# Products of ones beside the small products, another order in the first layer, and a longer ring

## The chip, the core and the metric

The kernel runs on one core of one Trainium2 chip. The core has TensorE (PE in the profile; its weight loads are PEld), VectorE (DVE), ScalarE (ACT), GpSimd (POOL) and SyncE (SP), which issues most transfers. Results of TensorE land in eight banks of PSUM. The metric is the device time of an execution in microseconds, from the first to the last instruction and a little around it; lower is better.

## The reference

Agent attention over B = 4 batches of N = 11,456 tokens with C = 128 channels and 49 agents, followed by a mixture of E = 8 experts with F = 1,024 hidden units, of which each token uses the one with the largest gate.

```python
s = scale * (agents @ k.T);  a2k = softmax(s over tokens);  agent_v = a2k @ v      # 49 x 128 per batch
x = softmax(scale * (q @ agents.T) over agents) @ agent_v                          # N x 128 per batch
logits = x @ w_gate;  e = argmax(logits)
out = softmax(logits)[e] * sigmoid(x @ w_output_gate)[e] * (relu(x @ w1[e]) @ w2[e])
```

All of it is fp32.

## The kernel before, in words

Tokens are worked on in units of 1,024 (11 per batch and a last one of 192); a unit is up to eight blocks of 128 tokens. Three kinds of **small products** in fp32 stand for the attention, eight to a unit: `ks` (key scores, block by agents, 50 columns), `av` (the weighted sum of v, accumulated over a unit) and `qs` (query scores). After the last `ks` of a batch the maximum over tokens is found (`km_t`, `km_r`), the weights `ev` of a unit are made by a subtraction on DVE or POOL and an exponential on ACT, and `av` follows. After the last `av`, `fold` finds the expert that most tokens of the batch will take (product `ga`, index `ei`), fetches its w1 and w2 (`w1t`, `w2t`), multiplies the agents' values by w1 (`aw`) and splits the result into fp16 parts `w`; `gates` makes the gate's weights (`bn`, `g`, then `lg` per unit).

The **main stream** goes over 92 tiles of up to 512 tokens. The first layer, `mm1(i, hf)`, makes four of a tile's eight chunks of 128 hidden units, one in each of PSUM banks 0 to 3 (G4 = 4), as fp16: a full product of 128 rows (`own_`, against the turned query weights x1) and a product of the 19 rows that are left (`rest`, against x2). The four small ones sit at partitions 0, 32, 64 and 96 and so run side by side in TensorE's row groups. `relu` brings a chunk out of its bank: ACT writes hh (fp16 of the ReLU), DVE writes hl (the rest of it), and the bank is released. hh and hl are rings of `RING` buffers each. The second layer, `mm2(i, k, f)`, multiplies hh and hl of chunk f by w2 into a bank y; `finish` and `store` sum and store it.

The order is made when the program is built. A model clock (`Clock`) holds a time for each engine; streams (generators) wait until their next instruction fits, and `tick(heavy, light)` lets at most `heavy` fp32 and `light` other TensorE instructions of the streams in. `main_stream` chooses between `mm1` and `mm2`: `mm2` when the first layer is more than `OFF` chunks ahead, `mm1` when banks 0 to 3 are free and the ring has room. Before the first `mm1` (`clk.started` false) and in gaps `idle` runs: it ticks, and it issues a filler, a product of fp16 ones into a free bank (`warm`), while the columns that the model has streamed in the last 3,413 ns are under a limit. The model counts an fp32 column four times:

```python
            n = _free(outs[0]) * (4 if ins[0].dtype == F32 and ins[0].shape[0] else 1)
            self.recent.append((t + cost, n * ins[0].shape[0] / 128.0))
```

At the start 36 fillers are issued outright. Loads of k, q and v go to `LARGE` places of 4 KB per partition; the turned weights x1 and x2 go to `SMALL` places of their own, or to large ones while more than `KEEP` of those are free. All instructions are recorded by one helper, so the profile gives them line 193.

Of the kernel before, what the change touches and what calls it, by code (L numbers as in the profile page):

```python
# [16 lines left out]
P = 128  # L17
# [3 lines left out]
UNITS = [(u * 1024, 128, 8) for u in range(11)] + [(11264, 96, 2)]  # L21
# [3 lines left out]

YS = 2

LARGE, SMALL, KEEP = 10, 8, 5
PHASES = [(0, 3, 13, 384), (3, 1, 1, 128)]
NG = B * E  # L30
BIG = 1048576.0
# [3 lines left out]
G4 = 4  # L35
# [207 lines left out]
def agent_attention_top1_moe(ctx, tc, qT, kT, v, aT, wg, wo, w1, w2, cst, out):  # L243
    nc = tc.nc
    clk = Clock()
    ACT, DVE, POOL = Engine(clk, "ACT", nc.scalar), Engine(clk, "DVE", nc.vector), Engine(clk, "POOL", nc.gpsimd)
    PE, SY = Engine(clk, "PE", nc.tensor), Engine(clk, "SP", nc.sync)
# [17 lines left out]
    def n_free():  # L265
        return sum(banks[k][0] for k in others)
# [4 lines left out]
    def first_free():  # L271
        return min((when_free(banks[k]), k) for k in others if banks[k][0])

    def bank(name, dt=F32, w=512, k=None):

        k = last[0] = first_free()[1] if k is None else k
        t = ps.tile([P, w], dt, tag=f"b{k}", bufs=1, name=name)
        banks[k][1] = t.name
        return t

    def hold(long=False):

        k = last[0]
        banks[k][0] = False
        if long:
            long_held.append((k, banks[k][1]))
        return k
# [4 lines left out]
    def idle_bank():  # L292
        free = [(when_free(x), k) for k, x in enumerate(banks) if x[0]]
        return min(free)[1] if len(free) > 1 and min(free)[0] <= clk.now() else None

    def group_free():

        if not all(banks[k][0] for k in range(G4)):
            return None
        return max(when_free(banks[k]) for k in range(G4))  # L300

    def wait_free(long=False):
        while True:
            long_held[:] = [x for x in long_held if not banks[x[0]][0] and banks[x[0]][1] == x[1]]
            if n_free() > (1 if clk.started else 0) and not (long and len(long_held) > 1) and first_free()[0] <= clk.now() + 50.0:
                return
            yield None
# [8 lines left out]
    def load_constants():  # L316
        SY.dma_start(kc, cst)
        SY.dma_start(wgo[:, 0:E], wg)
        SY.dma_start(wgo[:, E:2 * E], wo)
        for t in gss:  # L320
            POOL.tensor_copy(t[:, 0, 16:17], own)
# [8 lines left out]
    own = kc[:, K_OWN:K_OWN + 1]  # L330
    dup = kc[:, K_DUP:K_DUP + 1]
    idle_x = cp.tile([P, 256], F16, name="idle_x")
    idle_w = idle_x[:, 0:P]
# [9 lines left out]
    for i in range(4):  # L343
        t = cp.tile([P, 8, P], F16, name=f"e16_{i}")
        e16s.append(t)
    avd = []
    for i in range(2):
        t = cp.tile([P, 2, P], F32, name=f"avd_{i}")
# [3 lines left out]
    for i in range(2):  # L352
        t = cp.tile([P, 2, 18], F16, name=f"gs_{i}")
# [3 lines left out]
    for i in range(2):  # L357
        t = cp.tile([P, E, NCOL], F32, name=f"oht_{i}")
# [63 lines left out]
    mains = [0]  # L422
# [4 lines left out]
    def spawn(g, prio=2):  # L427
        streams.append([prio, len(streams), g, None])
        streams.sort(key=lambda x: x[0])

    def tick(heavy=1, light=2):

        clk.slots = [heavy, 0]
        for x in list(streams):
            if x[3] is not None and x[3][0] == "PE" and clk.can(x[3], x[0]):
                step(x)
        clk.slots = [0, light]
        for x in list(streams):
            while x[2] is not None and (x[3] is None or clk.can(x[3], x[0])):
                step(x)  # L440
                if x[3] is None:
                    break
        streams[:] = [x for x in streams if x[2] is not None]

    def step(x):
        try:
            x[3] = next(x[2])
        except StopIteration:
            x[2] = x[3] = None

    def idle():
        t = clk.vt["PE"]
        tick(*((1, 2) if clk.started else (1, 4)))
        k = idle_bank()
        if mains[0] == 0 and clk.columns(t) < (WARM if clk.vt["PE"] == t else 3600) and k is not None:

            PE.matmul(bank("warm", k=k)[:, 0:P], idle_w, idle_w, start=True, stop=True)
        elif clk.vt["PE"] == t:
            clk.vt["PE"] += 40.0

# [28 lines left out]
    def scored(item):  # L489
        places[held.pop(item)][0] = True  # L490
# [16 lines left out]
    def loads():  # L507
        for n, item in enumerate(ITEMS):
# [5 lines left out]
            if n == 1:  # L514
                load_constants()

    def scores(item, name):
        kind, b, u = item
        base, pp, nt = UNITS[u]
        while item not in parts:  # L520
            yield None
        yield from wait_free(True)
        x = parts.pop(item)
        s = bank(name)
        mark = hold(True)
        for t in range(nt):
            yield from PE.q.matmul(s[0:pp, t * A2:(t + 1) * A2], x[:, t * pp:(t + 1) * pp], at[:, b, :], start=True,
                                   stop=True)
        scored(item)
        return s, mark  # L530

# [77 lines left out]
    def v_unit(b, u):  # L609
        base, pp, nt = UNITS[u]  # L610
        item = ("v", b, u)
        while b not in K or u not in K[b] or item not in parts:
            yield None
        if u == 0:
            K[b]["av"] = wk.tile([P, A2], F32, name=f"avs{b}", tag="avs")
        yield from wait_free()
        avp = bank(f"av{b}_{u}")
        mark = hold()
        avo = avp[:, 0:A2]
        x = parts.pop(item)  # L620
        e = K[b].pop(u)
        for t in range(nt):
            sl = slice(t * C, (t + 1) * C)
            last_ = t == nt - 1
            yield from PE.q.matmul(avo, x[0:pp, sl], e[:, t, :], start=(t == 0), stop=last_)
        scored(item)
        K[b]["v"] += 1
        if b == 0 and u == NU - 4:
            others[:] = range(G4, 8)
        spawn(v_rest(b, u, avo, mark))  # L630

    def v_rest(b, u, avo, mark):
        av = K[b]["av"]
        while K[b]["av_n"] < u:
            yield None
        if u == 0:
            yield from DVE.q.tensor_copy(av, avo)
        else:
            yield from DVE.q.tensor_tensor(av, av, avo, op=ALU.add)
        release(mark)  # L640
        K[b]["av_n"] += 1
        if u == NU - 1:
            spawn(fold(b), -1)
# [179 lines left out]
    def q_unit(b, u):  # L823
        s, mark = yield from scores(("q", b, u), f"qs{b}_{u}")
        spawn(q_rest(b, u, s, mark))
# [3 lines left out]
    def roomy(me, n):  # L829

        if me < n:
            return True
        b, u = tiles[max(mains[0] - 1, 0)][0:2]
        return NU * b + u > me - n and rests[me - n] > 1
# [146 lines left out]
    def small_products():  # L981
        for kind, b, u in ITEMS:
            while kind == "q" and not roomy(NU * b + u, AHEAD):
                yield None
# [6 lines left out]
            for h in range((nt + 3) // 4):  # L991
                tiles.append((b, u, h, pp, min(4, nt - 4 * h)))
    NT = len(tiles)
    OFF = 6
    RING = 12
    H = {}
    Y = {}
    done, summed = set(), set()

    def mm1(i, hf):  # L1000


        b, u, h, pp, n = tiles[i]
        w = pp * n
        own_, rest = state[b]["w"][hf]
        x1, x2 = (x[:, 512 * h:512 * h + w] for x in X1[b, u])
        p = []
        for g in range(G4):
            p.append((bank(f"h{i}_{hf}_{g}", k=g), hold()))
            rows = slice(32 * g, 32 * g + AR)  # L1010
            PE.matmul(p[g][0][:, 0:w], rest[rows, g * P:(g + 1) * P], x2[rows, :], start=True, stop=False)
        for g in range(G4):
            PE.matmul(p[g][0][:, 0:w], own_[:, g * P:(g + 1) * P], x1, start=False, stop=True)
            spawn(relu(i, G4 * hf + g, *p[g]), 0)
            if g == G4 - 1 and hf == 1 and 4 * h + n == UNITS[u][2]:
                for x in ("x1", "x2"):
                    scored((x, b, u))
            tick()

    def relu(i, f, p, mark):  # L1020
        b, u, h, pp, n = tiles[i]
        w = pp * n
        hh = wk.tile([P, 512], F16, name=f"hh{i}_{f}", tag="hh", bufs=RING)
        hl = wk.tile([P, 512], F16, name=f"hl{i}_{f}", tag="hl", bufs=RING)
        yield from ACT.q.activation(hh[:, 0:w], p[:, 0:w], AF.Relu)
        yield from DVE.q.scalar_tensor_tensor(hl[:, 0:w], p[:, 0:w], 0.0, hh[:, 0:w], op0=ALU.max, op1=ALU.subtract)
        release(mark)
        H[i, f] = hh, hl
# [52 lines left out]
    def main_stream():  # L1081
# [3 lines left out]
        while m2 < len(second_):  # L1085
            can1 = can2 = False
            now = clk.now()
            if m1 < len(first_) and G4 * (m1 + 1) - freed <= RING and group_free() is not None and group_free() <= now + 20.0:
                i, hf = first_[m1]
# [4 lines left out]
            if (i, f) in H:  # L1094
                vv = state[tiles[i][0]]["vv"]
                can2 = len(vv) > f // 4 and clk.at([H[i, f][1], vv[f // 4]]) <= now
                can2 = can2 and (f > 0 or n_free() > 1)
            if can2 and (G4 * m1 > NB * i + (NB * k + f) / (tiles[i][4] // 2) + OFF or not can1):
                mm2(i, k, f)
# [11 lines left out]
        while streams:  # L1111
            idle()
# [312 lines left out]
                return stop.value  # L1425

    AHEAD = 5
    WARM = 6000
    WARM0 = 36
    LOW = POOL  # L1430
# [79 lines left out]
```

## Time and profile before

| | |
|---|---|
| median of 3 runs | 1107.53 us (1099.12 to 1108.6) |
| the profiled execution | 1105.42 us |
| its span | 1103.7 us |
| busy: PE, PEld, DVE, ACT, POOL | 1062.5, 874.1, 869.6, 594.1, 273.6 us |
| mean granted TensorE clock | 0.954 |
| first main product (h) | 98.34 us from the start |

A row of a timeline gives start and length in us, the engine, the operation with output and inputs (buffer numbers left out), its shape and how many; in brackets the idle time ahead of it and who ended it. A row of a stretch gives its bounds and length, and for each engine the busy time and the instructions that touch it, then the granted clock as a share, the busy share of the DMA engines and GB/s. A row of waits names who waited for whom, the sum in us, how often, and the longest.

### The profile page before, as it was taken

How to read it: one execution, taken by the hardware profiler on the slowest of the kernel's cores; microseconds unless marked ns; L12 is line 12 of the kernel's file. 1: busy time of each engine (PE TensorE's matmuls, PEld its weight loads, DVE VectorE, ACT ScalarE, POOL GpSimd, SP SyncE). 2: the span in 40 equal slices, each digit the busy share in tenths (PEclk: the TensorE clock that was granted, in tenths of full speed). 3: DMA queues.
4: the chain of work that ended last, by engine and by line, in shares of the span. 5: the costliest groups of instructions: out<-in, count | busy, mean ns of one | idle time of the engine just before them, and what ended most of it. 6: DMA issues, size and time to landing. Idle time of an engine off the chain costs nothing. (4 is left out here: it accounts for less than half of the span.)

```text
span 1103.7 us, 27308 instructions
## 1 busy us (share of the span) xinstructions
PE 1062.5 (96%) x10516; PEld 874.1 (79%) x10516; DVE 869.6 (79%) x2344; ACT 594.1 (54%) x1396; POOL 273.6 (25%) x440
## 2 busy tenths in 40 slices
PE   9999979999999999999999999999899989999996
PEld 9997858787778878888688878877676767878885
DVE  2626869898988898988988899888987979857652
ACT  2205636556655565665655566566555545655552
POOL 0300213232112122322112222231122344621121
PEclk9557989999999999999999999999999989999998
DMA  9527683444536634445455544455212364545340
GB/s 345 180 31 285 167 145 121 112 136 133 158 88 158 183 105 118 147 127 150 119 145 166 161 113 121 112 166 149 60 45 74 52 168 69 144 137 167 124 123 29
DMA packets 108817, 147.11 MB, mean 133 GB/s; under 512 B 61128, under 2 KB 71548, under 8 KB 108682
## 3 DMA queue, kind: packets, MB, share of 16 engines
q1 hardware_dynamic: 107338, 143.83, 46.6%
q0 software_dynamic: 1344, 1.49, 0.8%
q8 instruction: 83, 1.36, 0.5%
q14 instruction: 52, 0.43, 0.1%
HBM read 91.86 MB, written 35.17 MB: 115 GB/s over the span
## 5 line engine op out<-in xcount | busy, mean ns | idle before, releaser
L193 PE MATMUL y<-vv,hh 128*128 128x256 f16 (+1 forms) x2880 | 585.3, 275 | 8.8 <-DVE os L193 3.7
L193 PE MATMUL y<-vv,hl 128*128 128x128 f16 (+1 forms) x2880 | 531.0, 220 | 0.1
L193 DVE SCALAR_TENSOR_TENSOR hl<-h,hh 128x512 f16<-128x512 f32 (+1 forms) x736 | 447.4, 666 | 91.9 <-ACT hh L193 91.2
L193 ACT ACTIVATE hh<-h 128x512 f16<-128x512 f32 (+1 forms) x736 | 373.2, 590 | 230.9 <-PE h L193 229.5
L193 PEld LDWEIGHTS <-hl 128*128 128x128 f16 (+1 forms) x2880 | 318.3, 111 | 16.8 <-issue 4.3
L193 PEld LDWEIGHTS <-hh 128*128 128x128 f16 (+1 forms) x2880 | 290.4, 101 | 48.6 <-issue 3.2
L193 PE MATMUL h<-x_ld,w 19*128 19x512 f16 (+1 forms) x1472 | 296.0, 382 | 7.6 <-DVE hl L193 7.3
L193 PEld LDWEIGHTS <-w 19*128 19x128 f16 x1472 | 91.0, 102 | 111.8 <-issue 86.4
L193 POOL TENSOR_TENSOR os<-os,smt 128x512 f32<-128x512 f32 (+1 forms) x92 | 94.3, 1025 | 270.4 <-issue 213.5
L193 PE MATMUL av<-ev,v_ld 128*128 128x50 f32 x720 | 124.6, 287 | 0.0
L193 PEld LDWEIGHTS av<-ev,v_ld 128*128 128x128 f32 x720 | 122.4, 227 | 2.3 <-issue 1.0
L193 PEld LDWEIGHTS qs<-at,q_ld 128*128 128x128 f32 x720 | 116.3, 200 | 8.1 <-issue 0.3
L193 PE MATMUL qs<-at,q_ld 128*128 128x50 f32 x720 | 116.1, 256 | 0.3 <-DVE s_s L193 0.2
L193 PE MATMUL ks<-at,k_ld 128*128 128x50 f32 x720 | 106.3, 259 | 0.0
L193 PEld LDWEIGHTS ks<-at,k_ld 128*128 128x128 f32 x720 | 104.6, 196 | 1.9 <-issue 0.3
L193 ACT COPY ys<-y 128x256 f32<-128x256 f32 x180 | 68.0, 378 | 50.9 <-PE y L193 50.0
L193 DVE TENSOR_TENSOR os<-y,ys 128x256 f32<-128x256 f32 x180 | 74.6, 414 | 22.3 <-ACT ys L193 13.3
L193 POOL TENSOR_TENSOR e<-ef,e 128x392 f16<-128x392 f32 (+1 forms) x48 | 41.6, 867 | 160.2 <-ACT e L193 150.8
L193 POOL TENSOR_TENSOR ev<-S,km_o 128x400 f32<-128x400 f32 (+1 forms) x44 | 40.4, 918 | 145.3 <-PE av L193 103.3
L193 POOL TENSOR_SCALAR smt<-lT,i 128x8 f32<-128x8 f32 (+1 forms) x48 | 15.0, 313 | 125.3 <-DVE lT L193 102.3
L193 PE MATMUL lh<-lxs,lw 128*128 128x128 f32 x224 | 44.5, 286 | 0.6 <-ACT lxs L193 0.6
L193 ACT COPY S<-ks 128x400 f32<-128x400 f32 (+1 forms) x48 | 22.6, 473 | 40.4 <-PE ks L193 40.1
(197 smaller groups left out, 996.0 us busy)
## 6 DMA issues: line engine op xcount, KB each, us to landing
q_ld<-qT SPq DMA_DIRECT2D x44, 512.0 KB
v_ld<-v SPq DMA_DIRECT2D x44, 512.0 KB
out<-os SPq DMA_DIRECT2D x88, 256.0 KB
k_ld<-kT SPq DMA_DIRECT2D x43, 512.0 KB
lw<-w SPq DMA_DIRECT2D x28, 512.0 KB
efd<-ef SPq DMA_DIRECT2D x44, 200.0 KB
x_ld<-x_ld SPq DMA_DIRECT2D x176, 38.0 KB
w1t<-w SPq DMA_DIRECT2D x8, 256.0 KB
```

Source lines behind the costliest of these rows:

```text
L193: return getattr(self.eng, op)(*a, **k)
```

## The change

Three things. Ahead of the main stream, each `ks` and `qs` product, and each `av` product but a unit's last, is followed by a product of fp16 ones of 112 columns into unused columns of the same bank; fillers have 256 columns instead of 128, and one limit goes from 3,600 to 4,400. In `mm1` the four full products come first, with a tick after the first three, then the four products in row groups, then the four ReLU streams are started. `RING` goes from 12 to 16 chunks and `OFF` from 6 to 8; the room for it comes from two load places (`LARGE` 10 to 8, `KEEP` 5 to 4).

```diff
-LARGE, SMALL, KEEP = 10, 8, 5
+LARGE, SMALL, KEEP = 8, 8, 4
...
-        if mains[0] == 0 and clk.columns(t) < (WARM if clk.vt["PE"] == t else 3600) and k is not None:
-            PE.matmul(bank("warm", k=k)[:, 0:P], idle_w, idle_w, start=True, stop=True)
+        if mains[0] == 0 and clk.columns(t) < (WARM if clk.vt["PE"] == t else 4400) and k is not None:
+            PE.matmul(bank("warm", k=k)[:, 0:2 * P], idle_w, idle_x, start=True, stop=True)
...
+    def beside(t, own):
+        if not clk.started:
+            PE.matmul(t[:, 512 - SIDE:512], idle_w, idle_x[:, 0:SIDE], start=own, stop=own)
...
                                   stop=True)
+            beside(s, True)
...
             yield from PE.q.matmul(avo, x[0:pp, sl], e[:, t, :], start=(t == 0), stop=last_)
+            if not last_:
+                beside(avp, False)
...
-    OFF = 6
-    RING = 12
+    OFF = 8
+    RING = 16
...
         for g in range(G4):
             p.append((bank(f"h{i}_{hf}_{g}", k=g), hold()))
+            PE.matmul(p[g][0][:, 0:w], own_[:, g * P:(g + 1) * P], x1, start=True, stop=False)
+            if g < G4 - 1:
+                tick()
+        for g in range(G4):
             rows = slice(32 * g, 32 * g + AR)
-            PE.matmul(p[g][0][:, 0:w], rest[rows, g * P:(g + 1) * P], x2[rows, :], start=True, stop=False)
+            PE.matmul(p[g][0][:, 0:w], rest[rows, g * P:(g + 1) * P], x2[rows, :], start=False, stop=True)
         for g in range(G4):
-            PE.matmul(p[g][0][:, 0:w], own_[:, g * P:(g + 1) * P], x1, start=False, stop=True)
             spawn(relu(i, G4 * hf + g, *p[g]), 0)
-            if g == G4 - 1 and hf == 1 and 4 * h + n == UNITS[u][2]:
-                for x in ("x1", "x2"):
-                    scored((x, b, u))
-            tick()
+        if hf == 1 and 4 * h + n == UNITS[u][2]:
+            for x in ("x1", "x2"):
+                scored((x, b, u))
+        tick(0)
...
+    SIDE = 112
```

The order on TensorE near the end of the first batch's key scores, before (`ks_10` is unit 10, `warm` a filler, `idle_x` the ones):

```order
L193 MATMUL ks_10_461<-at,k_10_ld 128x50 x4
L193 LDWEIGHTS idle_x
L193 MATMUL warm<-idle_x 128x128
L193 MATMUL ks_10_461<-at,k_10_ld 128x50
L193 LDWEIGHTS idle_x
L193 MATMUL warm<-idle_x 128x128
L193 MATMUL ks_10_461<-at,k_10_ld 128x50 x3
L193 MATMUL ks_11_480<-at,k_11_ld 96x50 x2
L193 MATMUL qs_0_488<-at,q_0_ld 128x50 x5
L193 MATMUL km_t<-kc,mx_200 50x128
```

And the same place in the changed kernel:

```order
L193 MATMUL ks_10_481<-at,k_10_ld 128x50
L193 LDWEIGHTS idle_x
L193 MATMUL ks_10_481<-idle_x 128x112
L193 MATMUL ks_11_504<-at,k_11_ld 96x50
L193 LDWEIGHTS idle_x
L193 MATMUL ks_11_504<-idle_x 128x112
```

Each small product now has a ones product of its own behind it, in its own bank, and the fillers between them are gone. In the whole, 217 ones products stand ahead of the first h (114 beside ks, 25 beside qs, 78 beside av) and 88 fillers in place of 150; the same number of small products, and of every other kind, stands ahead of it as before.

A first-layer group on TensorE in the first batch's tile 20, before (`h20_0_2` is tile 20, half 0, bank 2; x20 and x10 are x2 and x1 of batch 0; w0_0 holds the weights of the row groups and w0_1 those of the full products):

```order
L193 MATMUL h20_0_2_5053<-x20_10_ld_3813,w0_0_1024 128x512
L193 LDWEIGHTS w0_0_1024
L193 MATMUL h20_0_3_5055<-x20_10_ld_3813,w0_0_1024 128x512
L193 LDWEIGHTS w0_1_1036
L193 MATMUL h20_0_0_5049<-x10_10_ld_3811,w0_1_1036 128x512
L193 LDWEIGHTS w0_1_1036
L193 MATMUL h20_0_1_5051<-x10_10_ld_3811,w0_1_1036 128x512
L193 MATMUL qs1_2_5061<-at_72,q1_2_ld_3547 128x50
L193 LDWEIGHTS w0_1_1036
L193 MATMUL h20_0_2_5053<-x10_10_ld_3811,w0_1_1036 128x512
L193 MATMUL qs1_2_5061<-at_72,q1_2_ld_3547 128x50
```

And in the changed kernel the end of the same group, from the last full product on (`lg1_1` are gate products of the next batch, `x11_1` its turned weights):

```order
L193 LDWEIGHTS w0_1_1108
L193 MATMUL h20_0_3_5130<-x10_10_ld_3886,w0_1_1108 128x512
L193 LDWEIGHTS w0_0_1093
L193 MATMUL h20_0_0_5110<-x20_10_ld_3888,w0_0_1093 128x512
L193 LDWEIGHTS w0_0_1093
L193 MATMUL h20_0_1_5118<-x20_10_ld_3888,w0_0_1093 128x512
L193 LDWEIGHTS w0_0_1093
L193 MATMUL h20_0_2_5123<-x20_10_ld_3888,w0_0_1093 128x512
L193 LDWEIGHTS w0_0_1093
L193 MATMUL h20_0_3_5130<-x20_10_ld_3888,w0_0_1093 128x512
L193 LDWEIGHTS x11_1_ld_5043
L193 MATMUL lg1_1_5116<-gs_1_93,x11_1_ld_5043 128x36
```

The products in row groups moved from the head of the group to its end, with nothing between them; small fp32 products stand between the full ones in both, and behind the group now only fp16 ones. Before, 174 of the 184 groups stand where the first layer is six chunks ahead of the second, and 147 stand eight steps of the second layer (calls of `mm2`) behind the group before. Now 143 stand at eight chunks ahead and 31 at five to seven, and the steps between groups are 7 to 9 for 125 of them and 3 to 6 for 40.

Between `ga` and the first `aw` of the first batch 38 fillers of 128 columns stood; now it is 17 of 256, with the same small products.

## The prediction

> **What bounds the kernel now.** I read the page's busy times and slices first, then the stages by time, then the order of TensorE's instructions ahead of the main stream, then the waits.
>
> ```profile
> span 1103.7 us, 27308 instructions
> PE 1062.5 (96%) x10516; PEld 874.1 (79%) x10516; DVE 869.6 (79%) x2344; ACT 594.1 (54%) x1396; POOL 273.6 (25%) x440
> PEclk9557989999999999999999999999999989999998
> ```
>
> TensorE is busy nearly all the time, but its clock is granted at half in the second to fourth of the 27.6 us slices. The stages say which part of the program that is (columns: busy us of PE, PEld, DVE, ACT, POOL, then granted clock, DMA share, GB/s):
>
> ```profile
> 25.00:50.00 25.00, 24.52 (x139) 24.23 (x139) 14.82 (x34) 6.48 (x14) 6.57 (x8) 0.58 0.67 217
> 50.00:75.00 25.00, 25.00 (x124) 25.00 (x124) 8.57 (x21) 2.43 (x5) 3.26 (x4) 0.50 0.35 45
> 75.00:100.00 25.00, 24.24 (x166) 20.92 (x166) 10.71 (x41) 8.71 (x22) 0.24 (x1) 0.70 0.75 282
> 100.00:125.00 25.00, 24.80 (x212) 19.52 (x211) 22.71 (x72) 15.18 (x35) 4.15 (x10) 0.84 0.38 104
> 125.00:150.00 25.00, 20.85 (x226) 19.00 (x224) 17.50 (x54) 11.09 (x28) 5.09 (x10) 0.93 0.97 205
> 600.00:700.00 100.00, 98.89 (x1066) 81.79 (x1067) 89.17 (x230) 59.28 (x136) 27.66 (x44) 1.00 0.49 134
> ```
>
> From 25 to 75 us PE and its weight loads are full while DVE, ACT, POOL and, from 50 us on, the DMA engines are far from it: this prelude is bound by TensorE at half clock. The main stream (600 to 700) is bound by TensorE at full clock, with DVE close behind. So whatever brings the first main product forward shortens the whole, since the change leaves the main stream's set of products as it was. The places in the prelude, in order of time:
>
> ```profile
> 11.18 0.22 PE L193 MATMUL warm<-idle_x 128*128 128x128 f16 x1
> 11.23 3.73 PE L193 MATMUL ks<-at,k_ld 128*128 128x50 f32 x32
> 14.79 0.22 PE L193 MATMUL warm<-idle_x 128*128 128x128 f16 x1
> 14.85 0.38 PE L193 MATMUL ks<-at,k_ld 128*128 128x50 f32 x2
> ...
> 27.77 1.28 PE L193 MATMUL qs<-at,q_ld 128*128 128x50 f32 x10
> 29.53 0.38 PE L193 MATMUL km_t<-kc,mx 128*50 128x128 f32 x1 [0.48 <-DVE mx L193]
> 31.42 0.66 PE L193 MATMUL km_r<-km_d,ones 50*128 50x50 f32 x2
> 36.02 7.01 PE L193 MATMUL av<-ev,v_ld 128*128 128x50 f32 x32
> 42.83 0.31 PE L193 MATMUL warm<-idle_x 128*128 128x128 f16 x1
> 42.93 0.61 PE L193 MATMUL av<-ev,v_ld 128*128 128x50 f32 x2
> ...
> 75.80 2.75 PE L193 MATMUL qs<-at,q_ld 128*128 128x50 f32 x12
> 78.34 0.56 PE L193 MATMUL ga<-wgs,ones 128*128 128x8 f32 x2
> 87.89 1.10 PE L193 MATMUL aw<-w1t,avd 128*128 128x512 f32 x2
> 98.34 0.61 PE L193 MATMUL h<-x_ld,w 19*128 19x512 f16 x4
> ```
>
> A small fp32 product is two records. At full clock 16 of them take 14.79 - 11.23 = 3.56 us, **0.2225 us** each; at half clock 42.83 - 36.02 = 6.81, **0.426** each. A filler in between costs 14.85 - 14.79, about **0.055**, at full clock and **0.10** at half.
>
> Why did the clock fall? The granted clock changes on a grid of 3.41 us; these are stretches of that grid:
>
> ```profile
> 19.01:22.42 3.41, 3.41 (x33) 3.41 (x32) 1.52 (x4) 0.82 (x2) 0.00 (x0) 1.00 1.04 407
> 22.42:25.83 3.41, 3.41 (x34) 3.41 (x33) 1.57 (x4) 0.73 (x3) 0.00 (x0) 1.00 1.01 399
> 25.83:29.25 3.42, 3.22 (x31) 3.09 (x30) 1.81 (x6) 1.04 (x3) 0.00 (x0) 1.00 1.05 417
> 29.25:32.66 3.41, 3.13 (x15) 2.97 (x15) 1.76 (x6) 0.00 (x0) 0.18 (x1) 0.50 0.97 368
> 83.86:87.27 3.41, 3.39 (x38) 3.23 (x36) 1.29 (x6) 0.49 (x1) 0.00 (x0) 0.50 0.95 335
> 87.27:90.69 3.42, 3.42 (x31) 2.19 (x28) 0.60 (x4) 2.03 (x7) 0.00 (x0) 1.00 1.02 406
> 97.51:100.93 3.42, 3.42 (x19) 2.53 (x19) 3.17 (x9) 2.53 (x4) 0.00 (x0) 0.50 0.95 377
> 104.34:107.75 3.41, 3.41 (x17) 1.43 (x16) 1.54 (x7) 1.47 (x4) 0.30 (x1) 0.50 0.92 220
> ```
>
> I count streamed columns as the kernel's own clock does (200 for a small product, 100 a record; 128 for a filler). Of the records in a stretch, those that start in it give 3,000 in the first (30 small ones) and 3,256 in the second: the clock stayed. The third has 27 small ones and two fillers, 2,956: half clock follows. With a product each 0.426 us a stretch holds some 1,600, and the clock stays low until the dense fillers before 87.27 (3,552). So on this trace the gate goes by density, with its limit near 3,000 per 3.41 us, and the small products alone (0.2225 us for 200 columns: 3,068) sit on that limit.
>
> **The change, part by part.** The sum is against the profiled execution: 1,105.42 us, 1.7 more than its span, and 2.1 under the median of the runs (1,107.53).
>
> *Ones beside the small products.* 114 + 25 + 78 of them stand ahead of the first main product, for 62 fewer fillers. A ones product of 112 columns has its own weight load; I price it as the filler of 128, 0.055 us at full clock. A pair is 312 columns in 0.2775 us, 3,837 per stretch; in the value sums, where seven of eight carry one, 3,758. The margin over 3,000 allows a pause of about 0.7 us per stretch.
>
> 1. Key scores, 90 products, 7.35 to 27.77 us at full clock already: 90 x 0.055 = 5.0 more, ten fillers fewer (0.55). **+4.4.** Nothing hides it: PE is full there, and the loads, at 407 GB/s in the stretch above 1.3 us for 512 KB, are faster than a unit's eight pairs (2.2).
> 2. From the last key score to the first value sum, 8.25 us. The wait on the maximum (km_t) stays. Four query products between km_t and km_r go from 0.43 to 0.28: -0.6. Behind km_r the order has seven more pairs, one small product and three 256-column fillers, some 2.7 us, where 4.6 stood. What is late next is the weights of the first unit:
>
> ```profile
> 33.90 0.54 ACT L193 ACTIVATE ev<-ev 128x400 f32<-128x400 f32 x1 [0.53 <-DVE ev L193]
> ```
>
>    It ends at 34.44, 3.0 behind km_r, so 3.1 remain: -1.5. Together **-2.1**, with a pause of 0.2 to 0.4 us, inside the margin.
> 3. Value sums, 90 products, 36.02 to 75.80 us: 39.8. At full clock 90 x 0.2225 + 78 x 0.055 = 24.3, and 0.3 for the product of the sums' total: 24.6. **-15.2.** The cover's next limit is DVE, 8.57 us busy for 7.5 units in the 50 to 75 row, 1.1 a unit against 2.2 for PE; not reached. Two load places fewer: the ninth unit's load waits until the first is summed, and it is used some 15 us later, against the 1.3 us above for a transfer.
> 4. Six query products ahead of the gate product ga: 2.54 becomes 1.7. **-0.9.**
> 5. From ga to the first h, 20.0 us: chains over DVE, ACT and a fetch of weights that the gate's answer starts.
>
> ```profile
> 80.48 0.96 SPq L193 DMA_DIRECT2D w1t<-w  x2
> ```
>
>    The first product on those weights, aw, stands 9.5 us behind ga; ahead of it, mostly at half clock, are 38 fillers and ten small products. By the new order and full clock that stretch is about 6.3. Behind aw the chain aw, whi, w is DVE's and ACT's and was at full clock; 17 ones are added there. I take -2.7 of the 3.2, with -5 and +1 as ends. **-2.7.**
>
> Sum of the prelude: 4.4 - 2.1 - 15.2 - 0.9 - 2.7 = **-16.5**: the first h at about 82 us in place of 98.3.
>
> 6. The main stream began at half clock (97.51 to 107.75). With fillers of 256 columns ahead of it the stretch before is dense. At half clock 9.4 us hold 4.7 us of work; DVE is at 22.71 of 25 there and would take some of it back. **-4**, between -2 and -4.7.
>
> *Order in the first layer, ring of 16.* No instruction is added. Each group still crosses twice between full products and products in row groups, once each way, so I take the crossings at nothing. What moves: h of all four banks is complete only at the group's end, so ReLU of the first bank starts three full products later (0.65 us); and the group asks for its banks one after the other, where the four row products asked for all at once. Two groups of before show what that asking costs:
>
> ```profile
> 642.79 1.41 PE L193 MATMUL h<-x_ld,w 19*128 19x512 f16 x8
> 644.04 0.27 PE L193 MATMUL y<-vv,hh 128*128 128x256 f16 x1
> ...
> 646.77 0.73 PE L193 MATMUL h<-x_ld,w 19*128 19x512 f16 x3
> 647.73 1.34 PE L193 MATMUL h<-x_ld,w 19*128 19x512 f16 x5 [0.23 <-DVE hl L193]
> 648.91 0.27 PE L193 MATMUL y<-vv,hh 128*128 128x256 f16 x1
> ```
> ```profile
> PE h L193 <- DVE hl L193: 7.3, 21, 1.7
> DVE hl L193 <- ACT hh L193: 91.2, 93, 3.8
> ```
>
> Undisturbed 1.25 us, late 2.14: 0.89 lost, of which 0.23 shows as a wait. At 21 places that is an estimate of 19 us in the whole. Asking 0.65 us later for the last bank can save up to two thirds of it, 13, where DVE is behind with other work, and nothing where the bank's own chain is late, since that chain also starts 0.65 later. In the new order the groups stand unevenly, nine steps of the second layer apart and then fewer, instead of eight: by the model's own times banks come free just in time. On the other side stands DVE's wait for hh: 0.65 at each of 93 places would be 60 us, of which DVE's idle tenth (89.17 of 100) absorbs most; I bound the loss by 20. Between -13 and +20 I take **-3**, nearest the row of 7.3 that is seen.
>
> *Places 8 for 10, kept 4 for 5.* Loads stand at 134 GB/s in the main stream against 407 above; I take nothing, with -4 to +4 for the waits at 125 to 150 us, where PE lacks 4.2 us.
>
> Total: -16.5 - 4 - 3 = -23.5, so 1,105.4 - 23.5 = **1,082 us**.
>
> **Rivals.** *The gate shuts anyway.* If one stretch in the passage of step 2 falls under 3,000, the clock halves, and then a pair takes 0.53 us: 312 columns each, 2,020 per stretch, and it can't open again before the dense fillers. Then the ones only cost: 4.4 + 1 (passage) + 78 x 0.10 - 1.2 (fillers gone) + 2 (behind the sums) = +14, and with the -3 **1,116 us, slower than before**. It decides at a pause of 0.7 us. For it: 0.48 us was enough in the third stretch. Against: that stretch had no ones, and the pauses I find are 0.2 to 0.4. Chance 0.08.
>
> *The ones do nothing to the gate*, because it goes by pauses and PE had hardly any: then the clock falls where it fell, and the time is the same 1,116. Against it: the first and third stretches differ by 0.19 us of busy time, and the stretches of 50 to 75 us have no pause at all and stay at half clock. Chance 0.03. The Trainium skill, "TensorE: Matmul & The Clock Gate", section "Why this matters for your kernels", asks for no idle gaps over some 3 us between bursts to keep the full clock; by that rule the clock should not have fallen at 29.25, where the trace shows 0.48 us idle, so the trace disagrees and I go by the stretches.
>
> *The main stream gives it back.* DVE, at 89 of 100, becomes the bound as each ReLU starts later: prelude as forecast, +12 to +20 in place of -3: 1,097 to 1,105, say 1,100. Chance 0.12.
>
> *The head start meets the transfers.* The queries' transposes and loads of the next batch fill the DMA engines from 81 us on; if the early main stream waits for them, as PE already does between 125 and 150, 12 to 16 of the gain is lost: 1,096. Chance 0.10, half of it within 1%.
>
> **How the numbers follow.** The forecast has 0.67: 1,066 (prelude -19, main -13, waits -4, clock -4) to 1,094. The range reaches on through the last two rivals to 1,102 and leaves out the two at 1,116 and the ends. About 1% is what a measurement of this kernel can tell from no change: against the median 1,107.5 that is 1,096.5 and 1,118.6. Faster: 0.67 + 0.05 + a little of the third rival, 0.76. Within: the rest of the two give-backs and half of the gate's cases, 0.17. Slower: 0.07.
>
> **What would show it.** Granted clock 1.0 from about 5 us to the first h; key scores 0.28 us a pair and some 25 us; value sums 24 to 25 us long; first h at 80 to 85 us; clock 1.0 in the first ten us of the main stream; DVE near 90 in its hundreds and waits of h on hl not above 7.3 us. Half clock anywhere between 30 and 60 us would make the forecast wrong, and so would more than 1,005 us from the first h to the end, which is what before takes.

## The result and the profile after

The changed kernel takes **1071.95 us** (median of 4 runs, 1070.46 to 1073.62) against 1108.07 (1099.12 to 1119.83) for the kernel before beside it: ratio 0.970, interval 0.964 to 0.976. The forecast was 1,082 in a range of 1,066 to 1,102. A second series on another chip gave 0.969 (0.966 to 0.972). The profiled execution took 1073.62 us, 31.8 less than that of before.

The head of the page of the changed kernel:

```profile
span 1071.6 us, 27654 instructions
PE 1033.2 (96%) x10671; PEld 840.9 (78%) x10671; DVE 859.9 (80%) x2344; ACT 592.6 (55%) x1396; POOL 275.2 (26%) x440
PEclk9999899999999999999999999999999998999998
```

The low digits of the second to fourth slice (5, 5 and 7) are gone. The same stretches as before the change (busy us of PE, PEld, DVE, ACT, POOL; granted clock, DMA share, GB/s):

```profile
25.00:50.00 25.00, 24.83 (x273) 24.39 (x272) 18.20 (x42) 8.58 (x18) 8.74 (x10) 1.00 0.83 244
50.00:75.00 25.00, 22.69 (x223) 19.82 (x222) 10.69 (x45) 4.79 (x14) 1.58 (x3) 1.00 0.71 161
75.00:100.00 25.00, 23.37 (x188) 18.46 (x189) 19.46 (x61) 14.46 (x34) 1.98 (x5) 0.86 0.76 223
100.00:125.00 25.00, 23.75 (x275) 21.80 (x274) 22.45 (x62) 14.54 (x33) 7.46 (x15) 1.00 0.73 156
125.00:150.00 25.00, 22.49 (x221) 17.10 (x222) 19.17 (x56) 13.25 (x33) 5.91 (x9) 0.86 0.70 165
600.00:700.00 100.00, 98.44 (x1055) 78.68 (x1054) 88.15 (x218) 60.02 (x136) 29.52 (x43) 1.00 0.44 117
```

From 25 to 75 us the clock is full and PE passes some 500 records where 263 passed before. The 0.86 between 75 and 100 us is the one flaw of the prelude. The places on PE, in order of time:

```profile
14.10 0.38 PE L193 MATMUL ks<-at,k_ld 128*128 128x50 f32 x2
14.31 0.21 PE L193 MATMUL ks<-idle_x 128*128 128x112 f16 x1
14.36 0.38 PE L193 MATMUL ks<-at,k_ld 128*128 128x50 f32 x2
...
31.64 0.38 PE L193 MATMUL qs<-at,q_ld 128*128 128x50 f32 x2
33.32 0.27 PE L193 MATMUL km_t<-kc,mx 128*50 128x128 f32 x1 [0.17 <-DVE mx L193]
37.36 0.42 PE L193 MATMUL av<-ev,v_ld 128*128 128x50 f32 x2
62.79 0.35 PE L193 MATMUL ga<-wgs,ones 128*128 128x8 f32 x2
69.17 2.81 PE L193 MATMUL aw<-w1t,avd 128*128 128x512 f32 x6 [0.20 <-DMA w1t<-w]
72.18 1.10 PE L193 MATMUL aw<-w1t,avd 128*128 128x512 f32 x2
75.53 0.42 PE L193 MATMUL ks<-at,k_ld 128*128 128x50 f32 x2 [2.25 <-DMA k_ld<-kT]
75.84 0.27 PE L193 MATMUL avn<-kc,avd 128*49 128x128 f32 x1
...
79.07 0.63 PE L193 MATMUL ks<-at,k_ld 128*128 128x50 f32 x2
79.49 0.30 PE L193 MATMUL ks<-idle_x 128*128 128x112 f16 x1
79.58 0.63 PE L193 MATMUL ks<-at,k_ld 128*128 128x50 f32 x2
85.03 0.38 PE L193 MATMUL h<-x_ld,w 128*128 128x512 f16 x1
```

A pair of a small product and its ones takes 14.36 - 14.10 = 0.26 us at full clock (0.267 by the mean of five pairs) and 79.58 - 79.07 = 0.51 at half. Counted by stage (the first key score starts 0.4 us later than before):

| | before | after | difference | forecast |
|---|---|---|---|---|
| 1 key scores, to the first qs | 20.4 | 23.9 | +3.5 | +4.4 |
| 2 passage, to the first av | 8.25 | 5.7 | -2.5 | -2.1 |
| 3, 4 value sums and six queries, to ga | 42.3 | 25.4 | -16.9 | -16.1 |
| 5 ga to the first h | 20.0 | 22.2 | **+2.2** | -2.7 |
| first h | 98.3 | 85.0 | -13.3 | -16.5 |
| main stream, first h to the end | 1005.3 | 986.5 | **-18.8** | -7 |

Step 5 is where the prelude misses. Behind aw, PE meets a key product of the second batch whose load has not landed, and avn, on which the weights w depend, is queued behind it. The grid stretches around that place:

```profile
71.10:74.52 3.42, 2.19 (x9) 0.88 (x7) 0.72 (x5) 0.29 (x1) 0.00 (x0) 1.00 1.01 357
74.52:77.93 3.41, 2.40 (x28) 2.40 (x28) 0.75 (x1) 2.21 (x7) 0.00 (x0) 1.00 1.02 398
77.93:81.34 3.41, 3.41 (x22) 3.41 (x22) 2.75 (x6) 1.90 (x4) 0.00 (x0) 0.50 1.03 415
```

After a pause the second holds 3,012 columns, and half clock follows until 84.76. So avn comes 6.7 us behind the first aw instead of 4.3, and h 9.2 behind avn instead of 6.1. In two further traces where the clock falls behind avn (the change again, ones and ring) h comes 10.0 and 10.1 us behind it, and in the three where it does not (ones alone and the two kernels with earlier keys) 5.7 to 6.3. SP had issued the load only behind the weights, some 7.6 us before it was there:

```profile
67.51 0.33 SPq L193 DMA_DIRECT2D w2t<-w  x1
67.95 0.84 SPq L193 DMA_DIRECT2D k_ld<-kT  x2
```

In the main stream the page has, for the first layer and its rest:

```profile
L193 PE MATMUL h<-x_ld,w 128*128 128x512 f16 (+1 forms) x1472 | 289.4, 379 | 12.1 <-DVE hl L193 11.5
L193 DVE SCALAR_TENSOR_TENSOR hl<-h,hh 128x512 f16<-128x512 f32 (+1 forms) x736 | 447.0, 667 | 85.3 <-ACT hh L193 84.2
```

PE waits 11.5 us for banks (before: 7.3), yet the main stream is shorter. Which part of the change did that, the whole can't say.

### The profile page after: what moved, and what is told of

Same layout as the page of the kernel before. It is cut to its first block, busy times and chain, and to the rows that moved or that the text cites. A ratio compares the mean times of both kernels' runs of the same rounds, so it can differ in the third digit from the quotient of the medians.

```text
span 1071.6 us, 27654 instructions
## 1 busy us (share of the span) xinstructions
PE 1033.2 (96%) x10671; PEld 840.9 (78%) x10671; DVE 859.9 (80%) x2344; ACT 592.6 (55%) x1396; POOL 275.2 (26%) x440
## 5 line engine op out<-in xcount | busy, mean ns | idle before, releaser
L193 PE MATMUL y<-vv,hh 128*128 128x256 f16 (+1 forms) x2880 | 593.0, 275 | 4.3 <-DVE w L193 3.1
L193 DVE SCALAR_TENSOR_TENSOR hl<-h,hh 128x512 f16<-128x512 f32 (+1 forms) x736 | 447.0, 667 | 85.3 <-ACT hh L193 84.2
L193 PEld LDWEIGHTS <-hh 128*128 128x128 f16 (+1 forms) x2880 | 284.7, 99 | 67.0 <-issue 37.1
L193 PE MATMUL h<-x_ld,w 128*128 128x512 f16 (+1 forms) x1472 | 289.4, 379 | 12.1 <-DVE hl L193 11.5
L193 PEld LDWEIGHTS <-w 128*128 128x128 f16 x1472 | 98.3, 103 | 105.0 <-issue 84.7
L193 PEld LDWEIGHTS qs<-at,q_ld 128*128 128x128 f32 x720 | 112.0, 190 | 7.0 <-DVE km_m L193 0.3
L193 PE MATMUL ks<-at,k_ld 128*128 128x50 f32 x720 | 111.4, 257 | 2.2 <-DMA k_ld<-kT 2.2
L193 PEld LDWEIGHTS ks<-at,k_ld 128*128 128x128 f32 x720 | 109.2, 195 | 5.5 <-DMA k_ld<-kT 3.1
L193 PE MATMUL av<-ev,v_ld 128*128 128x50 f32 x720 | 110.7, 251 | 0.0
L193 PEld LDWEIGHTS av<-ev,v_ld 128*128 128x128 f32 x720 | 107.6, 191 | 1.8 <-ACT ev L193 0.2
L193 PEld LDWEIGHTS <-idle_x 128*128 128x128 f16 x305 | 45.9, 158 | 2.7 <-DVE idle_x L193 1.1
```

Source lines behind the costliest of these rows:

```text
L193: return getattr(self.eng, op)(*a, **k)
```

## The experiments

Each kernel ran beside the kernel before on the same chip; ratios are against that. "Without ones" also puts back the fillers of 128 columns and the limit of 3,600; the ring is always RING, OFF and, to make room for it, the places.

| kernel | median us | ratio (interval) | first h | main stream | PE idle in it |
|---|---|---|---|---|---|
| before | | 1 | 98.3 | 1005.3 | 29.3 |
| ones alone | 1085.93 | 0.9765 (0.9676 to 0.9853) | 78.5 | 1006.5 | 30.6 |
| order alone | 1164.94 | 1.0459 (1.0352 to 1.0566) | 98.4 | 1070.7 | 71.5 |
| places alone | 1095.63 | 0.9935 (0.9904 to 0.9966) | 96.1 | 997.4 | 24.8 |
| ring | 1088.01 | 0.9765 (0.9645 to 0.9886) | 95.6 | 988.7 | 20.6 |
| order and ring | 1097.82 | 0.9856 (0.976 to 0.9952) | 98.4 | 1000.5 | 29.7 |
| the change (all) | 1071.95 | 0.9701 (0.964 to 0.9762) | 85.0 | 986.5 | 23.7 |
| the change, again | 1074.92 | 0.969 (0.966 to 0.9719) | 85.3 | 990.4 | 26.3 |
| ones and ring | **1065.84** | 0.964 (0.9612 to 0.9667) | 84.7 | 979.8 | 18.3 |
| the same, keys earlier | 1068.45 | 0.9622 (0.9585 to 0.966) | 81.6 | 985.5 | 19.8 |

First h, main stream (first h to the end) and PE's idle time in it are counted from the records of the profiled execution; the change run twice shows that a main stream differs by some 4 us between two of them.

The main stream can be cut into eighths by its second-layer products, which end 12.2 us before the execution does. In the second to fifth eighth the clock is full, but for one stretch in the kernel before and seven with the order alone, and there the parts can be told apart (us):

| kernel | first eighth | second to fifth | last three |
|---|---|---|---|
| before | 140.0 | 472.6 | 380.5 |
| ones alone | 135.6 | 472.3 | 386.4 |
| order alone | 143.2 | 511.7 | 403.7 |
| places alone | 133.0 | 470.1 | 382.1 |
| ring | 139.4 | 462.7 | 374.4 |
| order and ring | 143.0 | 465.9 | 379.3 |
| the change (all) | 134.3 | 465.4 | 374.6 |
| the change, again | 135.5 | 465.7 | 377.1 |
| ones and ring | 136.2 | 462.8 | 368.6 |

**Ones alone.** The ones, with the wider fillers and the limit of 4,400.

```diff
+            beside(s, True)
...
+                beside(avp, False)
```

> The ones products and the wider fillers alone; order of the first layer, ring and places as before. Theory (the ones hold the clock, the order and the ring act in the main stream alone): granted clock 1.0 from 6 to some 75 us, first h at 84 to 86 us as in the changed kernel (85.0), some 13 us earlier than before; main stream 1,000 to 1,005 us; time 1,089 to 1,094. Rival (the head start is what shortens the main stream too, because the early stalls fall away): main stream 987 to 993, time about 1,075.

Measured 1085.93, a little under the forecast: the first h came earlier (78.5) than the 84 to 86 of the theory. The main stream took 1006.5, so the rival's 987 to 993 is refuted. The prelude has step 5 as it was meant:

```profile
68.13 2.74 PE L193 MATMUL aw<-w1t,avd 128*128 128x512 f32 x6
71.07 1.10 PE L193 MATMUL aw<-w1t,avd 128*128 128x512 f32 x2
72.21 0.27 PE L193 MATMUL avn<-kc,avd 128*49 128x128 f32 x1
78.50 0.72 PE L193 MATMUL h<-x_ld,w 19*128 19x512 f16 x5
```

No wait for a load, full clock throughout, ga (62.1) to h 16.4 us: -3.6, inside the bounds of step 5. SP issued the same load here two us earlier:

```profile
65.99 0.82 SPq L193 DMA_DIRECT2D k_ld<-kT  x2
```

So the clock gives about 20 us of prelude; in the change 6.5 of them are lost again, 5.5 of these behind aw. What makes the load come earlier here was not isolated. The two load places more are one candidate, but narrow ones, below, has eight places like the change and doesn't wait for this load either.

**The order alone.**

```diff
+            PE.matmul(p[g][0][:, 0:w], own_[:, g * P:(g + 1) * P], x1, start=True, stop=False)
...
-            PE.matmul(p[g][0][:, 0:w], own_[:, g * P:(g + 1) * P], x1, start=False, stop=True)
```

> The order in the first layer alone (full products first); ring, places and prelude as before. Theory A (asking for the banks one after the other saves waits): no wait between the four row products, waits between full products instead, main stream 5 to 9 us shorter than before's 1,005, time 1,097 to 1,101. Rival (each ReLU starts 0.65 us later and a lead of six chunks doesn't cover it): the second layer waits for hl, main stream 5 to 15 us longer, 1,110 to 1,120.

Far slower than either expected. PE's waits, and one of them on DVE and on PE:

```profile
PE y L193 <- DVE os L193: 33.0, 26, 3.2
```
```profile
375.64 1.89 DVE L193 SCALAR_TENSOR_TENSOR hl<-h,hh 128x512 f16<-128x512 f32 x3 [0.21 <-ACT hh L193]
377.44 0.41 DVE L193 TENSOR_TENSOR os<-y,ys 96x256 f32<-96x256 f32 x1
```
```profile
377.90 0.27 PE L193 MATMUL y<-vv,hh 128*128 128x256 f16 x1 [2.71 <-DVE os L193]
```

All four ReLUs of a group now start at its end, so their hl stand on DVE one behind another; the sum os that frees a bank of the second layer is queued behind them, and PE starts that layer's next tile in the moment os ends (377.85). Before, this wait took 3.7 us in 4 places. Half clock comes on top: up to the last second-layer product 68 us of the main stream stand at half instead of 37, which is 16 us of the 65 lost; the idle time has 42.

**Places alone, and the ring with the places.**

```diff
-LARGE, SMALL, KEEP = 10, 8, 5
+LARGE, SMALL, KEEP = 8, 8, 4
```

> The kernel before with the places alone (LARGE 8, KEEP 4), ring and lead as before. Theory (what the ring-only kernel gained comes from the chunks): within 4 us of before, 1,104 to 1,112 us. Rival (the places do it: k and q stand less deep in SBUF, so the order of the loads and of the key scores changes): 1,085 to 1,095 us, with key scores of the main stream shorter by 5 us or more.

```diff
-    OFF = 6
-    RING = 12
+    OFF = 8
+    RING = 16
```

> The longer ring, the larger lead and two places fewer alone; order and prelude as before. Theory A: the lead covers the late ReLU of the new order only, so alone it does little: within 4 us of before, 1,102 to 1,110, with the waits between row products still near 18 us. Rival: the lead is what shortens the main stream: 8 to 12 us less, 1,094 to 1,098. Other rival: eight places hold up loads: 5 us more.

The places bring 0.65% (1095.63 us, between the two expectations), and with the chunks it is 2.35%. That is more than the rival for the ring forecast (1,094 to 1,098). The longer ring needs the room of the two places, so the chunks were not run alone. With the ring, PE's waits for banks in the old order are

```profile
PE h L193 <- DVE hl L193: 4.1, 14, 0.8
```

instead of 7.3, and its idle time in the main stream falls from 29.3 to 20.6 us.

**The order on top of the ring.** The change without the ones:

> The changed kernel without the ones products and with the narrow fillers of before: order and ring alone. If the three parts add up: first h at 98 us as before, main stream about 990, time 1,088 to 1,092, and order_only and ring_only together give this. If the ones also help the main stream through the clock at its start, 1,095.

Measured 1097.82, above both forecasts, with a main stream of 1000.5 instead of about 990.

And the change with the old order, the ones and the ring kept:

> The change without its new order of the first layer: the ones, the ring of 16 and the places stay, the row groups come ahead of the full products as before. Theory (with a ring of 16 the order itself costs, because all four ReLUs of a group start later and PE waits for banks): the prelude is the change's (first h at 78 to 85 us), the main stream is that of the ring alone (988.7 us) less the 4 us of a start at half clock: 1,060 to 1,068 us, with waits of h on hl of 3 to 6 us instead of 11.5. Rival (the order pays once the clock is open; its cost without the ones came only from the cold start): 1,072 to 1,080 us.

The order costs in both pairs: 0.9765 becomes 0.9856 without the ones, 0.964 becomes 0.970 with them. The intervals overlap in both, so the times alone don't settle it; the second to fifth eighth do. There the order costs 3.3 us without the ones and 2.6 with them, and PE's idle time grows by 3.6 and 3.4, where the change run twice differs by 0.3. The rest of the difference lies in the first and the last eighths, where the clock falls in some kernels and not in others, and may be chance. The row of PE's waits for banks, with order and ring, and then with ones and ring in the old order:

```profile
PE h L193 <- DVE hl L193: 12.4, 36, 3.9
```
```profile
PE h L193 <- DVE hl L193: 4.0, 13, 0.9
```

By the records, 18.4 us of pauses stood between the products in row groups before; with the new order none is left there, but 13.6 us stand between the full ones (order and ring); with ones and ring in the old order it is 14.7 between the products in row groups, so these pauses moved and did not grow. And DVE waits longer for hh; with ones and ring the page has 46 us in place of 84:

```profile
L193 DVE SCALAR_TENSOR_TENSOR hl<-h,hh 128x512 f16<-128x512 f32 (+1 forms) x736 | 447.1, 667 | 46.8 <-ACT hh L193 45.9
```

So the theory of that run holds: its time, its waits and, in the middle eighths, its cost of the order. At 1065.84 us, ones and ring lie **under both kernels**.

**What the gate goes by.** The gate is whatever grants TensorE the full or the half clock. First, narrower ones:

```diff
-    SIDE = 112
+    SIDE = 16
```

> The changed kernel with ones products of 16 columns in place of 112: as many products and weight loads, fewer columns. A pair is 216 columns; at 0.27 us a pair that is 2,730 per 3.41 us, under the limit of 3,000 that before's trace shows. Theory (the gate counts columns): the clock falls to a half within two stretches after the first ones products and stays there to the dense fillers near aw; key scores about 45 us, first h at 110 to 120, time 1,097 to 1,108. Rival (the gate counts pauses, or instructions): clock 1.0 as with 112 columns, first h at 85, time 1,072.

Measured 1076.96 (1075.89 to 1078.04), as the rival said. But the order of this kernel has 133 fillers of 256 columns ahead of the first h instead of 52: the model put back the columns that the ones had lost, and a stretch of the value sums still holds 3,444 to 4,296. The run doesn't tell columns from pauses or numbers. It does show that fillers can bring nearly all of the added columns: its first h is at 81.6. Wide fillers without any ones were not run.

With the fillers and the limit of before as well:

> The change with ones of 16 columns instead of 112 and the fillers of before (128 columns, limit 3,600): as many matmuls one behind another as in the change, but 216 columns a pair instead of 312. Theory (the gate counts streamed columns, limit near 3,000 in a stretch of 3.41 us): some 2,900 to 3,100 in a stretch, so the clock falls at the passage at the latest and stays at half through the value sums; first h at 92 to 102 us, 1,082 to 1,096 us. Rival (the gate goes by the number or density of matmuls): clock 1.0 up to ga, first h at 78 to 85 us, 1,068 to 1,076 us.

Measured 1119.21 (1118.44 to 1119.98), slower than before. The clock falls at once:

```profile
9.24:12.65 3.41, 3.41 (x42) 3.41 (x41) 0.67 (x2) 1.19 (x4) 1.57 (x4) 1.00 1.03 410
12.65:16.07 3.42, 3.42 (x23) 3.42 (x23) 0.76 (x3) 0.49 (x1) 0.00 (x0) 0.50 1.02 414
```

PE and its weight loads are full in the first of them, with more products than the change has in such a stretch, and no pause: but they stream 2,964 columns. It fell even earlier than I expected, and the first h came at 127.8 us, beyond the 92 to 102 of the theory. A full clock does not follow from the number of products or from having no pause; of the explanations put forward, streamed columns are left.

**Keys earlier.** Two more loads of the second batch's keys ahead of the weights:

```diff
-    FIRST_ITEMS = 2 * NU + 4
+    FIRST_ITEMS = 2 * NU + 6
```

> The changed kernel with two more loads ahead of the expert's weights (the second and third key unit of the next batch), nothing else. Theory (the wait of 2.25 us for that key unit delays the values' transpose and then the weights w, and thins the stretch at 74.5 so that the clock halves from 78 to 85): no wait at the key unit, clock 1.0 through to the first h, first h at 79 to 81 us instead of 85, time 1,066 to 1,069. Rival (the tail is the chain over ACT and DVE): first h at 83 to 85, time 1,070 to 1,073.

Measured 1073.87 (1073.24 to 1074.46), ratio 0.9639 (0.9547 to 0.9731), no gain on the change that can be told, and above the 1,066 to 1,069 of the theory. The wait for k_ld goes and h starts at 82.0, but w1 comes later:

```profile
70.33 1.48 PE L193 MATMUL aw<-w1t,avd 128*128 128x512 f32 x2 [1.29 <-DMA w1t<-w]
```

The main stream takes 989.4 us, no less than in the change's own two runs (986.5 and 990.4).

The same edit on ones and ring, run on one chip with the change itself:

> Ones, ring of 16 and places, the first layer as before, and two more loads of keys ahead of the weights, so that no key product waits for its load between aw and h. Theory (step 5's lost time is that wait and the half clock behind it): the wait of 1.6 us for k_ld goes, first h at 80 to 82 us instead of 84.7, 1,059 to 1,063 us. Rival (as with the change itself the loads take the place of w1, and the main stream gives the rest back): 1,064 to 1,067 us.

> The change itself, unaltered, beside the kernel before on the chip of the run that follows, so that the two can be compared there. Expected: 0.966 to 0.974 of before. If the version without the new order is really better by 5 to 7 us, its ratio is lower by 0.004 to 0.007.

The wait moved in the same way (1.28 us for w1t), h came at 81.6, and the time is no better than that of ones and ring without it: 1068.45 misses the theory's 1,059 to 1,063 and lies a little above the rival's 1,064 to 1,067. The comparison beside it held: all four runs of this version (1063.44 to 1068.95) lie under all four of the change (1072.85 to 1077.45), a ratio lower by 0.007. The two differ in the keys as well as in the order; on the change the earlier keys gained nothing that can be told.

**Half the ones**, behind every second small product, on the early keys:

> As early_keys, with a ones product behind every second small product only: 256 columns per 0.246 us on the mean, 3,550 per stretch. Theory (any density over 3,000 holds the clock, and each ones product costs 0.045 us on TensorE): clock 1.0 as there, key scores 22 us instead of 24, value sums 22 instead of 24, first h 4 us earlier than early_keys, time 1,062 to 1,065. Rival (the margin is too small for the passage between key scores and value sums): clock at a half from some 35 us, first h beyond 100, time over 1,085.

Three of five executions took 1073.3 us at a mean granted clock of 0.986, two 1102.3 and 1102.5 at 0.956 and 0.957; the profiled one is of the latter:

```profile
30.65:34.06 3.41, 3.13 (x30) 2.92 (x29) 2.62 (x9) 0.26 (x2) 0.01 (x1) 1.00 0.91 332
34.06:37.48 3.42, 3.42 (x21) 3.36 (x21) 1.98 (x4) 1.91 (x4) 1.91 (x3) 0.50 0.55 210
```

2,894 columns in the passage with a pause of 0.28 us, and the value sums stay at half clock. So the rival is right in two executions. In the other three the clock held, as the theory said, but the time of 1,062 to 1,065 was missed; why half the ones save nothing there isn't known, since there is no trace of such an execution.

## Why the prediction was right, point by point

- **The bound and the gate.** Right. The prelude was bound by PE at half clock, and the limit near 3,000 columns decided: 2,964 without a pause fell, 3,080 in 2.19 busy us (the stretch at 71.10) held, and 3,012 (at 74.52) fell, so the limit, or the count, is not sharp. One reading ahead was off: of the 0.48 us of pause that I put into the third stretch of before only 0.2 lie in it (3.22 busy of 3.42), and the rest lies behind the fall. The rival in which the ones do nothing is refuted by the ones alone, and the one in which the gate shuts anyway is real in kernels near the limit: with half the ones it shut in the passage in the traced execution (1,102; a second one was as long), with narrow ones and the narrow fillers at once (1,119). The change itself kept out of it in all eight of its runs.
- **Steps 1 to 4.** Right in each, and a little low in the sum: -15.9 against -13.8 forecast. A pair takes 0.267 us, not 0.2775, in the key scores and in the value sums alike.
- **Step 5.** Wrong, and outside its upper bound: +2.2 instead of -2.7. I looked at ga to aw, which came out as forecast (6.4 against 6.3), and took the chain behind aw as DVE's and ACT's. What failed is that I did not ask what PE meets there when it comes 16 us sooner: a key load whose issue stands on SP behind the weights that the gate's answer starts. That is 2.3 us of wait, and 3.1 more from avn to h, where half clock follows. Coming sooner is not enough for it: the ones alone come as soon, find the load there, and measured -3.6.
- **Step 6.** Its -4 is there: the ones alone shorten the way from the first h to the 384th y product from 88.9 to 84.4 us, -4.5, and the 100 to 125 row has clock 1.00; in the change it is 80.2. But with the ones alone the gain is gone by the end: the last three eighths take 386.4 us instead of 380.5, with 24 us at half clock instead of 14. No ones stand there, and what makes the clock fall more often isn't shown.
- **Step 7.** The term that was mis-sized. The forecast -3 for order and ring is about what the two do without the ones (main stream -4.8), by luck: it is the sum of two that I had mixed. The ring with its places alone measures -16.6 and the order +6.7 to +11.8 on top. In the second to fifth eighth, where the clock doesn't blur it, the ring has -9.9, of which the places alone show -2.5 where I took nothing, and the order +2.6 to +3.3. My argument for a gain of the order, that the bank wait is asked for later, is refuted by its row: 12.4 us of waits with it, 4.1 without. The bound +20 for the loss did not hold for the order alone (+65): I had not looked at what else stands on DVE behind four hl, the os. The change's -18.8 is more than its parts: ones alone measure +1.2, order and ring -4.8. The middle eighths are the same with and without the ones, and 13 of the 14 us between order and ring and the change stand in the first eighth (-8.7) and the last three (-4.7), with 20.5 us at half clock instead of 34.0 and 6 us less of idle time. The first of these is of the kind of step 6 (16.9 us at half clock there without the ones, 6.8 with them); the second has no cause shown.
- **The total.** Two errors cancelled in part, and that is luck: the prelude 3 us worse than forecast, the main stream 12 better. That leaves the 8 us by which the profiled execution lies under the forecast. Ones and main stream don't add up in full: 0.9765 and 0.9765 would make 0.954, ones and ring measure 0.964, and 6 of the missing 11 us are the first h at 84.7 instead of 78.5.
- **What would show it.** Right on the key scores, the value sums, DVE (88.15) and the main stream under 1,005. Wrong on the clock up to the first h (half from 77.93 to 84.76) and on the waits of h on hl (11.5, not up to 7.3); the first h is at the edge of 80 to 85.

## What to carry to other kernels

Where TensorE is full and its clock is still at half, count the columns it streams per stretch of the clock's grid, and fill up with wide cheap products rather than with many. When a stage gets faster, list what its engine meets next and who issues those loads, in the order of that queue. And take a change of several parts apart on the chip: here a part that cost 3 us of steady work, and 6 by the whole times, travelled unseen with two that gained.

## What the runs showed of the hardware

I had not expected the gate to be so blind to pauses and to the number of products. Over the fourteen traces I counted the columns of each stretch at full clock, with a record counted in the stretch in which it starts and weighted by its rows over 128. A stretch under 2,700 columns was followed by half clock in 68 of 69 cases, one of 2,700 to 3,000 in 18 of 24, of 3,000 to 3,300 in 6 of 47, and one above in 1 of 3,992. Pauses alone don't do it: in 197 of these last PE was idle for over 0.4 us, and the clock fell behind one of them. The Trainium skill, "TensorE: Matmul & The Clock Gate", section "What's actually happening", says that the clock is set by how busy PE has been in a window of about 3.4 us. The window agrees with the grid of 3.41 us; "busy" does not in the sense of the profile, since PE was busy for all of the stretch at 9.24 and the clock fell.
